# A layer norm, a spectral filter and a gated layer on one core: the filter's product one step later, its returns split, the last stage two tiles deep, fewer runs of zeros

## The chip, the cores and the metric

The kernel runs on one core of one Trainium2 chip. The metric is the time of the device in microseconds (us), start to end of one execution. A core has five engines with a queue of instructions each, taken in order: TensorE (PE; its weight loads are shown apart as PEld), VectorE (DVE), ScalarE (ACT), GpSimd (POOL) and SyncE (SP). Engines wait for each other through semaphores. DMA transfers are issued here by SP and by ACT.

## The reference

With x of 2048 rows and 512 columns in bf16, and xn the layer norm of x over its columns, the output is the sum of three terms:

```python
def _A_ref(x, w_r, w_i):
    X = rfft2(x.astype(float32))          # 2048 x 257, complex
    X = X * (w_r + 1j * w_i)
    return irfft2(X, s=(S, D)).astype(bfloat16)

def _B_ref(x, w_gate, w_up, w_down):      # 512 -> 1792 -> 512
    h = gelu(x @ w_gate) * (x @ w_up)
    return h @ w_down

xn = _layernorm(x)
return x + _A_ref(xn, w_r, w_i) + _B_ref(xn, w_gate, w_up, w_down)
```

## The kernel before

Everything is written out by hand. A small scheduler (`_Sched.op`) appends each operation to its engine's list in the order in which the program calls it, with the events that it must wait for; that order is each queue's order. A DMA counts on a named semaphore of its own.

The rows are held as 16 tiles of 128 rows, in four blocks of four. There are two streams of work, woven together.

*The gated layer* is made of units. A gate unit, `("g", block, fc)`, is two times four matmuls of 512 columns on PE (L504), a gelu on ACT (L516) and a product on DVE (L524) that writes hT. A down unit, `("d", block, n)`, is 14 matmuls (L552) that read all of the block's hT, and one add on DVE (L558). The units stand in one list, `fillers`, and `filler()` takes the next one. Gate units share a ring of three PSUM banks (0, 1, 2); down units of blocks 0 to 2 use bank 7, those of block 3 the gate units' ring.

*The spectral filter* is a two-dimensional transform made of matmuls, in stages:

- the first half, `unit_A` (L574) and `unit_d` (L600), one tile of 128 rows at a time through the buffers X1, stored to memory (`stage_p`) and read back in another order (`shuffle`);
- the middle, 16 units u of two groups each. `unit_B(u)`: two matmuls (L646), a copy by ACT into Xc (L651), and two DMAs on SP that write Xc with its halves of 64 partitions swapped into JX (L654). `product(u)`: three operations on DVE, M1 = Xc times wr (L663), JX = JX times wi (L664), M1 = M1 + JX (L665). `unit_c(u)`: two matmuls on M1 (L677), a copy by ACT into Vp (L682), and a store of Vp to memory (`stage_g`, L686) on SP;
- the return, `back(part)`: for each quarter of the groups, two DMAs (L696) that read `stage_g` back in another order into V, after the stores of that quarter;
- the last stage, per tile j: `unit_e(j)`, four matmuls (L710) and a copy by ACT into ZT (L715), and `unit_fin(j)`, four matmuls on ZT (L731), a copy by ACT (L738), two operations on DVE (L741, L742), one on DVE and one on POOL (L745), and the add into the output on POOL (L749). An output row is stored when both its down unit and its `unit_fin` have been added.

The middle runs in 19 steps. Step u has `unit_c(u-3)`, `unit_B(u)`, `product(u-2)`, one filler (steps 1 to 17), and after steps 8, 12 and 16 a return on ACT's queue; the last return is on SP's queue, behind the last step. Then come five fillers, and the last stage in 17 steps: `unit_e(j)`, `unit_fin(j-1)`, and a filler in steps 1 to 15. The four down units of block 3 are the end. `unit_B` and `unit_c` share four PSUM banks (3 to 6), two at a time. Xc and JX have three buffers, M1 and Vp two.

At the very start PE multiplies zeros by zeros into bank 7 (`warm_up`, L485) while the first rows are loaded and normed: NWARM gives the lengths of the runs, and each run after the first waits for an event of the norm (the statistics of tile 0, of tile 1, the reciprocal for both). The first real work are eight transposes (L441) and then gate units of 256 columns.

Of the kernel before, what the change touches and what calls it, by code (L numbers as in the profile page):

```python
# [7 lines left out]
ACT = mybir.ActivationFunctionType  # L8
ALU = mybir.AluOpType
# [5 lines left out]
HD = 256  # L15
NK = 257
FF = 1792
P = 128
NJ = 16
# [2 lines left out]
NFC = 14  # L22
NGG = 3
NX1 = 4
NWARM = (30, 6, 6, 5)
LN_EPS = 1e-5


# [123 lines left out]
class _Sched:  # L152
# [14 lines left out]
    def total(self, stream):  # L167
        return (stream, self.stream_cnt[stream])
# [59 lines left out]
def bass_parallel_sum__spectral_gfnet__glu_gated_geglu__prompt_kernel(  # L228
# [19 lines left out]
    sch = _Sched()  # L248

    with ExitStack() as es:  # L250

        def sb(name, shape, dt=BF16):
            return es.enter_context(nc.sbuf_tensor(name, shape, dt))
# [33 lines left out]
        V = bufB[:, :].rearrange("p (j c) -> p j c", j=NJ)  # L287
# [38 lines left out]

        streams = [("pe", 1), ("act", 1), ("dve", 1), ("pool", 1)]
        streams += [(n, 16) for n in ("x0", "x1", "x2", "x3", "xc1", "xc2", "xc3", "ident", "small", "fa", "eg", "wd", "wr", "wi",
                                      "w0", "w1", "w2", "w3", "dr0", "dr1", "perm1", "jx0", "jx1", "jx2", "vd0_0", "vd0_1", "vd1_0", "vd1_1", "vd2_0", "vd2_1", "vd3_0", "vd3_1", "perm2", "out")]
# [13 lines left out]
        spec = {}  # L343
# [29 lines left out]
        d2 = nc.dram_tensor("stage_g", [NG, P, NK], BF16).ap()  # L373
# [23 lines left out]
        ev_ag = {}  # L397
# [5 lines left out]
        ev_rstd = {}  # L403
# [160 lines left out]
        ev_X1 = {}  # L564
# [3 lines left out]
        def unit_A(j):  # L568
            slot, bdeps = ring_sp.alloc(1)

            def f_a(e):
                ins = None
                for r in range(4):
                    ins = e.matmul(sp_bank(slot)[:, r * P:(r + 1) * P], fold[:, r // 2, r % 2, j, :], AM[:, j, :], start=True, stop=True)  # L574
                return ins

            ev_p = sch.op("pe", f_a, deps=[ev_fa] + ev_fold[j // 4] + bdeps)
            spec["A_last"] = ev_p
            deps = [ev_p, X1_readers[j % NX1]]
            if j < 9:  # L580
                ev_X1[j] = sch.op("act", lambda e: e.activation(X1[j % NX1][:], sp_bank(slot), ACT.Copy), deps=deps)
            else:
                ev_X1[j] = sch.op("dve", lambda e: e.tensor_copy(X1[j % NX1][:], sp_bank(slot)), deps=deps)
            ring_sp.add_reader(slot, ev_X1[j])

        def clear_holes():
# [41 lines left out]
        Xc_readers = [[], [], []]  # L628
        JX_readers = [[], [], []]
        M_readers = [[], []]  # L630
        Vp_readers = [[], []]
        ev_Xc = {}
        ev_JX = {}
        ev_Y = {}
# [1 line left out]
        PARTS = ((0, 8), (8, 16), (16, 24), (24, 32))  # L636

        def unit_B(u):
            s3 = u % 3
            slot, bdeps = ring_sp.alloc(2)  # L640

            def f_b(e):
                ins = None
                for i in range(2):
                    g = 2 * u + i
                    ins = e.matmul(sp_bank(slot + i)[:, 0:NK], BM[:, 1 if g == 0 else 0, :], Tp[:, g, :], start=True, stop=True)  # L646
                return ins
# [3 lines left out]
            ev_Xc[u] = sch.op("act", lambda e: e.activation(Xc[s3][:], sp_pair(slot), ACT.Copy), deps=[ev_p] + Xc_readers[s3])  # L651
            ring_sp.add_reader(slot, ev_Xc[u], 2)
            for h in range(2):
                sch.op("sp", lambda e, h=h: e.dma_start(JX[s3][64 * h:64 * h + 64, :, :], Xc[s3][64 - 64 * h:128 - 64 * h, :, :]),  # L654
                       deps=[ev_Xc[u]] + JX_readers[s3], stream="jx%d" % s3)
            ev_JX[u] = total("jx%d" % s3)
            Xc_readers[s3] = [ev_JX[u]]

        def product(u):

            s2, s3 = u % 2, u % 3
            gs = slice(2 * u, 2 * u + 2)
            a = sch.op("dve", lambda e: e.tensor_tensor(M1[s2][:], Xc[s3][:], wr_sb[:, gs, :], ALU.mult), deps=[ev_Xc[u]] + M_readers[s2] + spec["wr"])  # L663
            b = sch.op("dve", lambda e: e.tensor_tensor(JX[s3][:], JX[s3][:], wi_sb[:, gs, :], ALU.mult), deps=[ev_JX[u], spec["neg"][u // 4]])  # L664
            ev_Y[u] = sch.op("dve", lambda e: e.tensor_tensor(M1[s2][:], M1[s2][:], JX[s3][:], ALU.add), deps=[a, b])  # L665
            Xc_readers[s3].append(a)
            JX_readers[s3] = [ev_Y[u]]

        def unit_c(u):
            s2 = u % 2  # L670
            slot, bdeps = ring_sp.alloc(2)

            def f_c(e):
                ins = None
                for i in range(2):
                    kind = 1 if 2 * u + i == 0 else 0
                    ins = e.matmul(sp_bank(slot + i)[:, 0:NK], CM[:, kind, :], M1[s2][:, i, :], start=True, stop=True)  # L677
# [4 lines left out]
            ev_v = sch.op("act", lambda e: e.activation(Vp[s2][:], sp_pair(slot), ACT.Copy), deps=[ev_p] + Vp_readers[s2])  # L682
            ring_sp.add_reader(slot, ev_v, 2)
            part = next(i for i, (lo, hi) in enumerate(PARTS) if lo <= 2 * u < hi)
            name = "vd%d_%d" % (part, s2)
            sch.op("sp", lambda e: e.dma_start(d2[2 * u:2 * u + 2].rearrange("g r k -> r g k"), Vp[s2][:]), deps=[ev_v], stream=name)  # L686
            Vp_readers[s2] = [total(name)]

        def back(part, eng):

            lo, hi = PARTS[part]
            ev = [total("vd%d_%d" % (part, i)) for i in range(2)]
            for pq in range(2):
                src = bass.AP(tensor=d2.tensor, offset=d2.offset + (lo * P + 16 * pq) * NK + pq,
                              ap=[[32 * NK, 4 * (hi - lo)], [NK, NJ], [1, HD]])
                sch.op(eng, lambda e, pq=pq, src=src: e.dma_start(V[4 * lo:4 * hi, :, pq * HD:(pq + 1) * HD], src),  # L696
                       deps=ev + [spec["A_last"]], stream="perm2")
            spec["perm2"] = total("perm2")

        ev_ZT = {}  # L700
# [213 lines left out]
```

## Time and profile before

| | us |
|---|---|
| runs | 186.41, 186.61, 186.67; median 186.61 |
| the profiled execution | 187.52 |
| its span, first to last instruction | 185.7 |
| PE busy in the stretch 60 to 78 (18.0 us) | 17.89 |
| PE busy in the middle, 78 to 124.5 (46.5 us) | 44.05 |
| of it 96 to 104 and 104 to 115 (8.0 and 11.0 us) | 6.98 and 10.04 |
| PE busy from 150 to 170 (20.0 us) | 19.84 |
| DVE, ACT, POOL busy in the middle (46.5 us) | 30.14, 25.97, 0.00 |
| DMA share in 84 to 96, 96 to 104, 104 to 115 | 0.40, 0.83, 0.63 |

A line of the profile's groups or of the order of time has a start and a duration in us, the engine, the line of the code, the operation, what is written and read with its shape, and in brackets the idle time of the engine before it and what ended it. "ACTq" and "SPq" are the engines' sequencers, which issue DMAs. Matmuls are pipelined: the start of one to the start of the next is its cost, and the duration shown is longer. The granted TensorE clock is 1.00 in each stretch that the profile reports, so the pace of the matmuls is read from their starts.

### The profile page before, as it was taken

What the parts mean: (1) busy time and instruction counts of PE and PEld (TensorE: products, weight loads), DVE (VectorE), ACT (ScalarE), POOL (GpSimd) and SP (SyncE); (2) the same over time, 40 slices, a digit from 0 to 9 for tenths busy, and PEclk for the clock granted to TensorE, in tenths of its full rate; (3) what the DMA queues carried; (4) which work ended last, traced back from release to release, by engine and by line L of the source; (5) the groups of instructions that cost most, each with busy time, mean ns of one, the idle gap of its engine ahead of it and who ended that gap; (6) DMA issues with size and microseconds to landing.
All of it is one profiled execution on the core that took longest, in us unless ns stands there. A gap on an engine that the chain in (4) does not pass through costs nothing.

```text
span 185.7 us, 3182 instructions
## 1 busy us (share of the span) xinstructions
PE 177.3 (95%) x1145; PEld 100.7 (54%) x1165; DVE 118.1 (64%) x252; ACT 88.6 (48%) x161; POOL 55.5 (30%) x54
## 2 busy tenths in 40 slices
PE   7999999999999999999999798999899999998994
PEld 6688555565655544545554453444455545554453
DVE  1767968799674636567585684733456858588221
ACT  2544446787463542267475472623453635465000
POOL 0064271373630000000000000000169778699500
PEclk9999999999999999999999999999999999999999
DMA  5999960999999584824349376545001021110001
GB/s 159 349 365 371 371 208 28 173 183 190 213 186 183 171 264 130 240 71 114 104 114 190 106 153 150 133 122 115 4 28 56 28 70 47 56 58 5 28 28 56
DMA packets 32224, 26.10 MB, mean 141 GB/s; under 512 B 2256, under 2 KB 31440, under 8 KB 32080
## 3 DMA queue, kind: packets, MB, share of 16 engines
q1 hardware_dynamic: 28368, 23.90, 49.4%
q10 hardware_dynamic: 3840, 2.00, 5.4%
q8 instruction: 9, 0.15, 0.3%
q14 instruction: 7, 0.06, 0.1%
HBM read 17.48 MB, written 6.30 MB: 128 GB/s over the span
## 4 chain that ended last, share of the span: by engine, by line
PE 82%; DMA 9%; DVE 4%; ACT 2%; issue 1%; SPq 1%; DVEq 0%
PE ps L504 46%; PE ps L552 23%; DMA JX<-Xc 7%; PE ps L441 2%; PE ps L731 2%; PE ps L574 2%; PE ps L600 2%; PE ps L710 2%; DMA x_sb<-in_A_x_dram 2%; PE ps L677 1%; DVE hT L524 1%; ACT Xc L651 1%; PE ps L485 1%; PE ps L646 1%; DVE M L665 1%
## 5 line engine op out<-in xcount | busy, mean ns | idle before, releaser
L504 PE MATMUL ps<-xnT,wu_sb 128*128 128x512 bf16 (+1 forms) x246 | 58.6, 361 | 0.1
L504 PE MATMUL ps<-xnT,wg_sb 128*128 128x512 bf16 (+1 forms) x233 | 56.4, 360 | 0.8
L524 DVE TENSOR_TENSOR hT<-ps,gg 128x512 bf16<-128x512 f32 (+1 forms) x62 | 39.5, 638 | 22.3 <-PE ps L504 21.1
L552 PE MATMUL ps<-wd_sb,hT 128*128 128x512 bf16 (+1 forms) x235 | 50.4, 367 | 0.8 <-DVE hT L524 0.6
L516 ACT ACTIVATE gg<-ps 128x512 bf16<-128x512 f32 (+1 forms) x62 | 34.4, 555 | 25.0 <-PE ps L504 23.9
L745 POOL TENSOR_TENSOR bufC<-bufC 128x256 bf16<-128x256 f32 x16 | 14.9, 931 | 86.5 <-DVE bufC L742 86.5
L504 PEld LDWEIGHTS ps<-xnT,wu_sb 128*128 128x128 bf16 x248 | 24.4, 99 | 24.3
L552 PEld LDWEIGHTS ps<-wd_sb,hT 128*128 128x128 bf16 x238 | 22.9, 98 | 23.4 <-DVE hT L524 0.8
L504 PEld LDWEIGHTS ps<-xnT,wg_sb 128*128 128x128 bf16 x248 | 23.2, 98 | 15.4 <-ACT xnT L450 0.2
L558 DVE TENSOR_TENSOR x_sb<-ps,x_sb 128x512 bf16<-128x512 f32 (+1 forms) x17 | 11.2, 660 | 24.2 <-PE ps L552 24.2
L465 POOL TENSOR_TENSOR bufC<-bufA 128x1024 bf16<-128x1024 bf16 x8 | 16.8, 2123 | 8.0 <-DVE bufA L423 8.0
L749 POOL TENSOR_TENSOR x_sb<-x_sb,bufC 128x512 bf16<-128x512 bf16 x16 | 18.5, 1154 | 2.3
L682 ACT ACTIVATE Vp<-ps 128x514 bf16<-128x514 f32 x16 | 9.6, 599 | 16.4 <-PE ps L677 14.3
L715 ACT ACTIVATE bufA<-ps 128x512 bf16<-128x512 f32 x16 | 9.4, 597 | 16.0 <-PE ps L710 16.0
L608 ACT ACTIVATE bufA<-ps 128x512 bf16<-128x512 f32 x16 | 11.9, 744 | 9.2 <-PE ps L600 9.2
L400 DVE BATCH_NORM_STATS2 st<-x_sb 128x6 f32<-128x512 bf16 x16 | 10.8, 678 | 3.1 <-DMA x_sb<-in_A_x_dram 3.1
L651 ACT ACTIVATE Xc<-ps 128x514 bf16<-128x514 f32 x16 | 9.4, 595 | 4.0 <-PE ps L646 4.0
L741 DVE TENSOR_TENSOR bufC<-bufC,ps 128x256 f32<-128x256 f32 x16 | 6.7, 421 | 6.4 <-ACT bufC L738 6.4
L664 DVE TENSOR_TENSOR JX<-JX,wi_sb 128x514 bf16<-128x514 bf16 x16 | 6.8, 424 | 5.7 <-DMA JX<-Xc 5.7
L677 PE MATMUL ps<-M,small 128*128 128x257 bf16 x32 | 6.2, 276 | 2.2 <-DVE M L665 2.2
L415 POOL TENSOR_SCALAR rstd<-ag 128x4 f32<-128x4 f32 (+1 forms) x4 | 1.6, 402 | 21.2 <-DVE ag L401 21.2
L745 DVE TENSOR_TENSOR bufC<-bufC 128x256 bf16<-128x256 f32 x16 | 7.2, 452 | 0.5
(42 smaller groups left out, 142.0 us busy)
## 6 DMA issues: line engine op xcount, KB each, us to landing
JX<-Xc SPq DMA_DIRECT2D x32, 64.2 KB, 2.3
stage_g<-Vp SPq DMA_DIRECT2D x16, 128.5 KB, 3.3
stage_p<-bufA SPq DMA_DIRECT2D x16, 128.0 KB, 7.8
bufC<-stage_p SPq DMA_DIRECT2D x4, 512.0 KB, 5.4
out_dram<-x_sb SPq DMA_DIRECT2D x15, 128.0 KB, 1.8
wd_sb<-in_B_w_down_dram SPq DMA_DIRECT2D x1, 1792.0 KB, 13.3
wr_sb<-in_A_w_r_dram SPq DMA_DIRECT2D x6, 257.0 KB, 6.5
wi_sb<-in_A_w_i_dram SPq DMA_DIRECT2D x6, 257.0 KB, 11.5
```

Of the source, the lines that this page charges most:

```text
L400: ev = sch.op("dve", lambda e: e.bn_stats(st[:, j, :], x_sb[:, j, :]), deps=[ev_x[j]])
L465: ev_hf[m] = [sch.op("pool", lambda e, t=t, op=op: e.tensor_tensor(half[:, m, t, :, :], rows[:, 0, :, :], rows[:, 1, :, :], op), deps=deps ...
L504: ins = e.matmul(gu_bank(slot)[:, 0:w], wsb[:, dc, fc * P:(fc + 1) * P], xnT[:, dc, b * 512 + a:b * 512 + a + w], start=(dc == 0), stop=(d ...
L516: ev_gg = sch.op("act", lambda e: e.activation(gg, gu_bank(gslot)[:, 0:w], ACT.Gelu_apprx_tanh), deps=[ev_gm] + gg_readers[s2])
L524: ev_h = sch.op("dve", lambda e: e.tensor_tensor(hT[hb][:, fc, a:a + w], gu_bank(uslot)[:, 0:w], gg, ALU.mult), deps=[ev_um, ev_gg] + hdeps)
L552: ins = e.matmul(bank(slot)[:, 0:w], hT[hb][:, fc, jj * P:(jj + 1) * P], wd_sb[:, fc, cs], start=(fc == 0), stop=(fc == NFC - 1))
L558: ev_a = sch.op("dve", lambda e, slot=slot, cs=cs: e.tensor_tensor(x_sb[:, j, cs], bank(slot)[:, 0:w], x_sb[:, j, cs], ALU.add), deps=[ev_ ...
L608: ev_T[j] = sch.op("act", lambda e: e.activation(dst, src, ACT.Copy), deps=[ev_p, tr[j]] + ev_hf[j // 4])
L651: ev_Xc[u] = sch.op("act", lambda e: e.activation(Xc[s3][:], sp_pair(slot), ACT.Copy), deps=[ev_p] + Xc_readers[s3])
L682: ev_v = sch.op("act", lambda e: e.activation(Vp[s2][:], sp_pair(slot), ACT.Copy), deps=[ev_p] + Vp_readers[s2])
L745: y = [sch.op(("dve", "pool")[h], lambda e, h=h, op=op: e.tensor_tensor(rS[s2][:, h * HD:(h + 1) * HD], yeS[s2][:, 0, :], yeS[s2][:, 1, :] ...
L749: ev_o = sch.op("pool", lambda e: e.tensor_tensor(x_sb[:, j, :], x_sb[:, j, :], rS[s2], ALU.add), deps=[a, b, ev_xn[j]] + ev_acc.get(j, []))
```

## The change

It has five parts.

1. The product of a unit comes three steps behind its transform and `unit_c` four: step u has `unit_c(u-4)`, `unit_B(u)`, `product(u-3)`. There are still 19 steps: step 16 has two products (13 and 14), step 17 one (15), step 18 two `unit_c` (14 and 15).
2. Xc and JX have four buffers and Vp three. The room for the fourth ones and for M1 comes from X1: one tile, `tmp`, holds X1's four buffers in the first half and afterwards M1, the fourth Xc and the fourth JX, as views.
3. A return's two DMAs are issued in two steps: after steps 9 and 10, 13 and 14, 17 and 18. The last return's two stay together on SP's queue.
4. The last stage runs `unit_fin(j-2)` beside `unit_e(j)`, in 18 steps, and the last down unit of block 2 stands behind all gate units of block 3 in the list of fillers, not before their last five.
5. The zeros are a run of 46, and one of 4 that waits for the reciprocal.

```diff
-NWARM = (30, 6, 6, 5)
+NWARM = (46, 4)
...
-        X1 = [sb("X1_%d" % i, [P, 512]) for i in range(NX1)]
+        tmp = sb("tmp", [P, 8 * NK])
...
-        Xc = [sb("Xc%d" % i, [P, 2, NK]) for i in range(3)]
-        JX = [sb("JX%d" % i, [P, 2, NK]) for i in range(3)]
-        M1 = [sb("M1_%d" % i, [P, 2, NK]) for i in range(2)]
-        Vp = [sb("Vp%d" % i, [P, 2, NK]) for i in range(2)]
+
+        X1 = [tmp[:, i * 512:(i + 1) * 512] for i in range(NX1)]
+        pairs = [tmp[:, i * 2 * NK:(i + 1) * 2 * NK].rearrange("p (a k) -> p a k", a=2) for i in range(4)]
+        M1 = pairs[0:2]
+        Xc = [sb("Xc%d" % i, [P, 2, NK])[:] for i in range(3)] + [pairs[2]]
+        JX = [sb("JX%d" % i, [P, 2, NK])[:] for i in range(3)] + [pairs[3]]
+        Vp = [sb("Vp%d" % i, [P, 2, NK]) for i in range(3)]
...
         def unit_B(u):
-            s3 = u % 3
+            s3 = u % 4
...
         def product(u):
 
-            s2, s3 = u % 2, u % 3
+            s2, s3 = u % 2, u % 4
...
         def unit_c(u):
-            s2 = u % 2
+            s2, sv = u % 2, u % 3
...
-        def back(part, eng):
+        def back(part, pq, eng):
 
             lo, hi = PARTS[part]
-            ev = [total("vd%d_%d" % (part, i)) for i in range(2)]
-            for pq in range(2):
-                src = bass.AP(tensor=d2.tensor, offset=d2.offset + (lo * P + 16 * pq) * NK + pq,
-                              ap=[[32 * NK, 4 * (hi - lo)], [NK, NJ], [1, HD]])
-                sch.op(eng, lambda e, pq=pq, src=src: e.dma_start(V[4 * lo:4 * hi, :, pq * HD:(pq + 1) * HD], src),
-                       deps=ev + [spec["A_last"]], stream="perm2")
+            src = bass.AP(tensor=d2.tensor, offset=d2.offset + (lo * P + 16 * pq) * NK + pq,
+                          ap=[[32 * NK, 4 * (hi - lo)], [NK, NJ], [1, HD]])
+            sch.op(eng, lambda e: e.dma_start(V[4 * lo:4 * hi, :, pq * HD:(pq + 1) * HD], src),
+                   deps=[total("vd%d_%d" % (part, i)) for i in range(3)] + [spec["A_last"]], stream="perm2")
             spec["perm2"] = total("perm2")
...
-        for n, ev in zip(NWARM, (None, ev_ag[0], ev_ag[1], ev_rstd[0])):
+        for n, ev in zip(NWARM, (None, ev_rstd[0])):
             warm_up(n, ev)
...
-                for n, at in enumerate((4, 7, 10, 13) if b < 3 else (3, 5, 7, 9)):
+                for n, at in enumerate((4, 7, 10, 13) if b < 3 else (3, 5, 7, 14)):
                     units.insert(at + n, ("d", b - 1, n))
...
         for u in range(19):
-            if u >= 3:
-                unit_c(u - 3)
+            for v in ((14, 15) if u == 18 else (u - 4,)):
+                if v >= 0:
+                    unit_c(v)
             if u < 16:
                 unit_B(u)
-            if 2 <= u < 18:
-                product(u - 2)
+            for v in {16: (13, 14), 17: (15,), 18: ()}.get(u, (u - 3,)):
+                if v >= 0:
+                    product(v)
             if 1 <= u < 18:
                 filler()
 
-            if u in (8, 12, 16):
-                back(u // 4 - 2, "act")
-        back(3, "sp")
+            if u in (9, 10, 13, 14, 17, 18):
+                back(u // 4 - 2, (u - 9) % 4, "act")
+        for pq in range(2):
+            back(3, pq, "sp")
         filler(todo["left"] - 15 - 4)
-        for j in range(NJ + 1):
+        for j in range(NJ + 2):
             if j < NJ:
                 unit_e(j)
-            if j >= 1:
-                unit_fin(j - 1)
+            if j >= 2:
+                unit_fin(j - 2)
             if 1 <= j < NJ:
                 filler()
         filler(todo["left"])
```

More of the change, by code (lines that the diff above doesn't have):

```diff
@@ L328, in bass_parallel_sum__spectral_gfnet__glu_gated_geglu__prompt_kernel @@
         streams += [(n, 16) for n in ("x0", "x1", "x2", "x3", "xc1", "xc2", "xc3", "ident", "small", "fa", "eg", "wd", "wr", "wi",
-                                      "w0", "w1", "w2", "w3", "dr0", "dr1", "perm1", "jx0", "jx1", "jx2", "vd0_0", "vd0_1", "vd1_0", "vd1_1", "vd2_0", "vd2_1", "vd3_0", "vd3_1", "perm2", "out")]
+                                      "w0", "w1", "w2", "w3", "dr0", "dr1", "perm1", "jx0", "jx1", "jx2", "jx3", "vd0_0", "vd0_1", "vd0_2", "vd1_0", "vd1_1", "vd1_2", "vd2_0", "vd2_1", "vd2_2", "vd3_0", "vd3_1", "vd3_2", "perm2", "out")]
         for name, inc in streams:
@@ L580, in unit_A @@
             if j < 9:
-                ev_X1[j] = sch.op("act", lambda e: e.activation(X1[j % NX1][:], sp_bank(slot), ACT.Copy), deps=deps)
+                ev_X1[j] = sch.op("act", lambda e: e.activation(X1[j % NX1], sp_bank(slot), ACT.Copy), deps=deps)
             else:
-                ev_X1[j] = sch.op("dve", lambda e: e.tensor_copy(X1[j % NX1][:], sp_bank(slot)), deps=deps)
+                ev_X1[j] = sch.op("dve", lambda e: e.tensor_copy(X1[j % NX1], sp_bank(slot)), deps=deps)
             ring_sp.add_reader(slot, ev_X1[j])
@@ L626, in negate @@
                 sch.op("dve", lambda e: e.tensor_scalar(w, w, -1.0, None, ALU.mult), deps=spec["wi"]))
-        Xc_readers = [[], [], []]
-        JX_readers = [[], [], []]
+        Xc_readers = [[] for _ in range(4)]
+        JX_readers = [[] for _ in range(4)]
         M_readers = [[], []]
-        Vp_readers = [[], []]
+        Vp_readers = [[], [], []]
         ev_Xc = {}
@@ L650, in unit_B @@
             spec["B_last"] = ev_p
-            ev_Xc[u] = sch.op("act", lambda e: e.activation(Xc[s3][:], sp_pair(slot), ACT.Copy), deps=[ev_p] + Xc_readers[s3])
+            ev_Xc[u] = sch.op("act", lambda e: e.activation(Xc[s3], sp_pair(slot), ACT.Copy), deps=[ev_p] + Xc_readers[s3])
             ring_sp.add_reader(slot, ev_Xc[u], 2)
@@ L659, in product @@
         def product(u):
-            s2, s3 = u % 2, u % 3
+            s2, s3 = u % 2, u % 4
             gs = slice(2 * u, 2 * u + 2)
-            a = sch.op("dve", lambda e: e.tensor_tensor(M1[s2][:], Xc[s3][:], wr_sb[:, gs, :], ALU.mult), deps=[ev_Xc[u]] + M_readers[s2] + spec["wr"])
-            b = sch.op("dve", lambda e: e.tensor_tensor(JX[s3][:], JX[s3][:], wi_sb[:, gs, :], ALU.mult), deps=[ev_JX[u], spec["neg"][u // 4]])
-            ev_Y[u] = sch.op("dve", lambda e: e.tensor_tensor(M1[s2][:], M1[s2][:], JX[s3][:], ALU.add), deps=[a, b])
+            a = sch.op("dve", lambda e: e.tensor_tensor(M1[s2], Xc[s3], wr_sb[:, gs, :], ALU.mult), deps=[ev_Xc[u]] + M_readers[s2] + spec["wr"])
+            b = sch.op("dve", lambda e: e.tensor_tensor(JX[s3], JX[s3], wi_sb[:, gs, :], ALU.mult), deps=[ev_JX[u], spec["neg"][u // 4]])
+            ev_Y[u] = sch.op("dve", lambda e: e.tensor_tensor(M1[s2], M1[s2], JX[s3], ALU.add), deps=[a, b])
             Xc_readers[s3].append(a)
@@ L681, in unit_c @@
             M_readers[s2] = [ev_p]
-            ev_v = sch.op("act", lambda e: e.activation(Vp[s2][:], sp_pair(slot), ACT.Copy), deps=[ev_p] + Vp_readers[s2])
+            ev_v = sch.op("act", lambda e: e.activation(Vp[sv][:], sp_pair(slot), ACT.Copy), deps=[ev_p] + Vp_readers[sv])
             ring_sp.add_reader(slot, ev_v, 2)
             part = next(i for i, (lo, hi) in enumerate(PARTS) if lo <= 2 * u < hi)
-            name = "vd%d_%d" % (part, s2)
-            sch.op("sp", lambda e: e.dma_start(d2[2 * u:2 * u + 2].rearrange("g r k -> r g k"), Vp[s2][:]), deps=[ev_v], stream=name)
-            Vp_readers[s2] = [total(name)]
-        def back(part, eng):
+            name = "vd%d_%d" % (part, sv)
+            sch.op("sp", lambda e: e.dma_start(d2[2 * u:2 * u + 2].rearrange("g r k -> r g k"), Vp[sv][:]), deps=[ev_v], stream=name)
+            Vp_readers[sv] = [total(name)]
+        def back(part, pq, eng):
             lo, hi = PARTS[part]
-            ev = [total("vd%d_%d" % (part, i)) for i in range(2)]
-            for pq in range(2):
-                src = bass.AP(tensor=d2.tensor, offset=d2.offset + (lo * P + 16 * pq) * NK + pq,
-                              ap=[[32 * NK, 4 * (hi - lo)], [NK, NJ], [1, HD]])
-                sch.op(eng, lambda e, pq=pq, src=src: e.dma_start(V[4 * lo:4 * hi, :, pq * HD:(pq + 1) * HD], src),
-                       deps=ev + [spec["A_last"]], stream="perm2")
+            src = bass.AP(tensor=d2.tensor, offset=d2.offset + (lo * P + 16 * pq) * NK + pq,
+                          ap=[[32 * NK, 4 * (hi - lo)], [NK, NJ], [1, HD]])
+            sch.op(eng, lambda e: e.dma_start(V[4 * lo:4 * hi, :, pq * HD:(pq + 1) * HD], src),
+                   deps=[total("vd%d_%d" % (part, i)) for i in range(3)] + [spec["A_last"]], stream="perm2")
             spec["perm2"] = total("perm2")
```

## The prediction

> **What bounds the kernel now.** I read the page first, for the share of TensorE, then the list of who waited for whom, kept to TensorE, then the order of time at each place where it waited.
>
> ```profile
> PE 177.3 (95%) x1145; PEld 100.7 (54%) x1165; DVE 118.1 (64%) x252; ACT 88.6 (48%) x161; POOL 55.5 (30%) x54
> ...
> PE ps L677 <- DVE M L665: 2.2, 3, 1.0
> ...
> PE ps L552 <- DVE hT L524: 0.6, 1, 0.6
> ...
> PE ps L731 <- ACT bufA L715: 0.5, 1, 0.5
> ```
>
> TensorE is busy 177.3 of 185.7 us, so only two things can shorten the run: its idle time and the time in which its matmuls are slow. The list (us in total, times, longest) has 2.2 us before three L677 products, 0.6 before the last down products, 0.5 before the first L731, and beside these only waits of the zeros (L485) at the start. Next, the order of time at a product wait.
>
> ```profile
> 96.43 0.93 ACTq L696 DMA_DIRECT2D bufB<-stage_g  x2
> 96.45 1.10 SPq L654 DMA_DIRECT2D JX<-Xc  x2
> ...
> 102.90 0.43 DVE L664 TENSOR_TENSOR JX<-JX,wi_sb 128x514 bf16<-128x514 bf16 x1 [2.42 <-DMA JX<-Xc]
> 103.36 0.43 DVE L665 TENSOR_TENSOR M<-M,JX 128x514 bf16<-128x514 bf16 x1
> 103.71 0.68 DVE L558 TENSOR_TENSOR x_sb<-ps,x_sb 128x512 bf16<-128x512 f32 x1
> 103.85 0.40 PE L677 MATMUL ps<-M,small 128*128 128x257 bf16 x2 [0.97 <-DVE M L665]
> ```
>
> ACT issues two returns (L696) in the same moment as SP issues the swap of one unit (L654). That swap lands after 5.2 and 5.9 us; the first swap, with no return near, took 2.0. VectorE waits 2.42 us for it and TensorE 0.97 after that. The second pair of returns (107.55) repeats it with 0.91; 0.30 is lost at the first product of all.
>
> **The change, part by part.**
>
> *Product three steps behind, four buffers, split returns.* The swap of unit u is issued up to 2.0 us into its step (second half at 96.95, step begun at 94.91) and multiplied some 1.15 us into the step of its product. Two ordinary steps of 2.17 us leave 3.5 us, and 5.9 does not fit: 2.4 us of waiting, as shown. With three steps, one of which holds a down product (3.46 us) for every unit near the first two pairs of returns, 6.9 us are left, so even an unsplit 5.9 fits. The first product gets a whole extra step. Gain 2.2, bounds 1.3 (one wait stays) and 2.2 (no more is there). The matmuls are the same, and the extra buffers cost no instruction. Splitting moves one DMA issue of each pair past one more step on ACT; the issue (0.3 to 0.6 us on ACT's sequencer) lies beside the running gelu.
>
> A rule of the Trainium skill speaks against the split: its page "DMA: Bandwidth & Descriptors", in "Issuing engines are not separate DMA queues", says that transfers of all issuing engines end up on the same 16 DMA engines and interleave. The 5.9 us of the swap on SP behind ACT's returns agrees. By that rule alone the split returns would slow twice as many swaps half as much and be worth nothing; the sum here gives the split nothing either, since the third step covers both.
>
> *The seam, steps 16 to 18.* The lag has to be made up: step 16 now has two products (units 13 and 14), step 17 the last, step 18 two L677 pairs. VectorE runs in order, and each step's gate product (L524) waits for TensorE. The spacing is that of these rows:
>
> ```profile
> 117.30 0.69 DVE L524 TENSOR_TENSOR hT<-ps,gg 128x512 bf16<-128x512 f32 x1 [0.70 <-PE ps L504]
> 117.91 0.42 DVE L663 TENSOR_TENSOR M<-Xc,wr_sb 128x514 bf16<-128x514 bf16 x1
> 118.24 0.42 DVE L664 TENSOR_TENSOR JX<-JX,wi_sb 128x514 bf16<-128x514 bf16 x1
> 118.69 0.43 DVE L665 TENSOR_TENSOR M<-M,JX 128x514 bf16<-128x514 bf16 x1
> ```
>
> L524 starts 0.21 after TensorE's step ends (117.09); then +0.61, +0.33, +0.45 to the three product operations, +0.35 from an L665 to the next operation (103.36 to 103.71). Let T be TensorE's start of step 16. VectorE: L524 of step 15 at T+0.21, product 13 from 0.82 (its L665 ends at 2.03), product 14 from 1.95 (ends 3.16), L524 of step 16 at 3.08, product 15 from 3.69, its L665 ends at 4.90. TensorE: L677 pair 0.22, gate and up products to 1.95; the next pair waits for 2.09; gate and up to 4.04; pair 14 to 4.26; pair 15 waits for 4.96 and ends at 5.18. Before, this stretch with one pair fewer ran from 117.09 to 121.36, 4.27 us; with the fourth pair 4.49. Cost 5.18 - 4.49 = 0.7. The bounds: 0.35 if half the queue hides, and 1.3, because the swap of unit 15 follows a return. It is multiplied at T+4.02, its second half is issued near T-0.55, and the swap that followed two returns by one step (109.7 to 110.2) took up to 5.2, which would be T+4.65, 0.6 late.
>
> *The last return.* It follows the last pair on SP and now competes with both returns of the third part. Before, the last store (122.26) took 2.7, the later half of the last return (125.35) landed 4.5 after its issue, at 129.9, and the last stage began at 131.29: 1.4 us of cover. After: from the last pair's start 1.05 to the store's issue, 3.4 for the store (the value of the one at 118.14, which had two returns behind it), 0.4 for the second issue, 4.5: 9.4 us. The last stage begins 10.15 after that start (121.14 to 131.29). Cover 0.8, cost 0. With the slowest store between returns (109.25, 5.8) it is 11.75, cost 1.6. Bounds 0 and 1.6; I take 0, by the nearer row. Third store buffers only end waits of ACT (1.6 us at 90.79) on which TensorE did not wait.
>
> *Two tiles ahead, and the last of block 2's down products moved to the end.*
>
> ```profile
> 131.72 1.09 ACT L715 ACTIVATE bufA<-ps 128x512 bf16<-128x512 f32 x2 [0.49 <-PE ps L710]
> 132.37 0.40 PE L731 MATMUL ps<-fa,bufA 128*128 128x128 bf16 x4 [0.47 <-ACT bufA L715]
> 170.22 0.68 DVE L524 TENSOR_TENSOR hT<-ps,gg 128x512 bf16<-128x512 f32 x1
> 170.96 1.25 PE L552 MATMUL ps<-wd_sb,hT 128*128 128x512 bf16 x5 [0.64 <-DVE hT L524]
> ```
>
> The first L731 now comes 3.02 us of down products later than the copy of its input: 0.5 gone. The last L524 gets the same 3.02 us of cover ahead of the final down products: 0.6 gone. What follows a step later is POOL's tail: two tiles of about 2.17 us behind the start of the final products, done some 5.3 us in, when the add for the last tile is 10.8 us in (170.96 to 181.76). Without that cover POOL's 2.17 would count in full.
>
> *Zeros: 46 and 4 for 30, 6, 6 and 5.*
>
> ```profile
> 0.97 3.38 PE L485 MATMUL ps<-hT 128*128 128x128 bf16 x30 [0.97 <-DVE hT L394]
> 4.98 2.15 PE L485 MATMUL ps<-hT 128*128 128x128 bf16 x17 [0.62 <-DVE ag L401]
> 8.84 1.06 PE L504 MATMUL ps<-xnT,wu_sb 128*128 128x256 bf16 x4
> 9.69 0.67 PE L504 MATMUL ps<-xnT,wg_sb 128*128 128x256 bf16 x4
> 10.19 0.60 PE L504 MATMUL ps<-xnT,wu_sb 128*128 128x256 bf16 x4
> 10.63 0.60 PE L504 MATMUL ps<-xnT,wg_sb 128*128 128x256 bf16 x4
> ```
>
> Four matmuls take 0.85 us from 8.84 and 0.44 from 10.19: the array reaches full pace near 9.7, some 4.7 us after work with no long gap began (4.98). The 46 zeros run at 0.11 each from 0.97 to about 6.0, unbroken for 5 us, before the reciprocal that the last four await (6.25), so nothing is delayed. If 4.7 us are what it needs, full pace is there before the real work; about 0.9 us of slow matmuls fall away, but the second piece of the up weights, issued at 3.59, lands 7.5 later, at 11.07, and its user started at 11.50: at most 0.43 gained. If instead the two new gaps (near 6.0 and before 7.16) make the count start anew at 7.16, full pace comes at 11.9, and 2.2 us at 0.48 lost per us cost 1.05. Bounds -0.43 and +1.05; I take -0.2, between nothing and the weights' limit.
>
> The Trainium skill's page "TensorE: Matmul & The Clock Gate" (section "Part 1: The HAM clock gate") describes a free-running window of about 3.4 us that must be busy. By it, a run of 5 us holds a whole window only for some phases, and the sum would move by anything from -0.43 to nothing for the phase drawn; no run here shows the window itself.
>
> **Sum.** -2.2 - 0.5 - 0.6 + 0.7 + 0 - 0.2 = -2.8. Against the profiled execution's 187.52 (185.7 of span, 1.8 around it) that gives 184.7. The median of the runs, 186.61, lies 0.9 lower; I carry the difference over: **183.8**.
>
> **Rivals.** *Seam and last return cost their upper ends* (chance 0.17): SP, ACT and the returns are closer together than before, which the 5.8 us store at 109.25 speaks for and the 3.4 at 118.14 against. +1.6 gives 185.4, with the late swap's 0.6 it is 186.0. *The clock comes later* (0.08): +1.05 instead of -0.2 gives 185.05. *The waits stay* (0.05): the third step covers nothing, because swaps land later than 6.9 us; no row is above 5.9. The 1.9 of the two waits come back: 185.7. *VectorE becomes the bound* (0.08), the slower side: M1 and the fourth Xc and JX lie in one shared tile at odd multiples of 1028 bytes. If the three product operations there took the 0.68 of the 512-wide copies from ps (L583) instead of 0.42, each product grows by 0.78 against 0.34 of idle per step; ten ordinary steps lose 4.4, the seam 2.3: 190.5. It is slower than before from 0.48 per product on (10 x (0.48 - 0.34) + 3 x 0.48 = 2.8). Against it: wr_sb and wi_sb are read at such multiples, and all 16 of each of L663 and L664 took 417 to 429 ns.
>
> **How the numbers follow.** The forecast has 0.62 (183.0 to 184.6 with its own terms). For 8 in 10 the range goes up into the first two rivals and down past the full 0.43 of the zeros: 182.9 to 185.6. A change within 0.2%, 0.37 us, can't be told from none. All cases but the last are faster by more; the last holds slower 0.07 and, with partial slowing, same 0.03; faster 0.90.
>
> **What would show it.** Right: no L664 wait for JX, L677 waits of 0.1 and 0.7 only in steps 17 and 18, no wait of L731 or of L552 for L524, four 256-wide matmuls in 0.44 us before 9. Wrong: an L710 wait for the last return, L663 to L665 above 0.43, or a slow pace beyond 10.

## The result, and the profile after

The changed kernel takes 183.42 us (median of 182.99 to 183.68, 4 runs) against 186.64 (186.41 to 186.92) for the kernel before: ratio 0.9824, 95% interval 0.9801 to 0.9848, so 3.2 us less. The prediction was 183.8 with a range of 182.9 to 185.6.

The page of the changed kernel (first line) and its list of TensorE's waits (us in total, times, longest); the line numbers have moved by 3, L677 is now L680, L664 is L667:

```profile
PE 175.1 (97%) x1148; PEld 99.8 (55%) x1168; DVE 117.3 (65%) x252; ACT 88.5 (49%) x161; POOL 55.5 (31%) x54
...
PE ps L488 <- DVE hT L397: 1.0, 1, 1.0
PE ps L680 <- DVE tmp L668: 0.5, 1, 0.5
PE ps L444 <- DVE bufA L426: 0.5, 1, 0.5
PE ps L507 <- DMA wu_sb<-in_B_w_up_dram: 0.5, 1, 0.5
```

Of the three waits of the product one is left, and it is at another place (the seam, below). The waits before the first L731 and before the last down products are gone. Two new ones have come at the start: the transposes (L444) wait for the normed rows, and a gate unit (L507) waits for the up weights.

The span fell by 4.5 us (185.7 to 181.2), more than the medians' 3.2. Cut at three marks that both traces have (lines as they were before), the first L646 (78.16 before, 76.98 after), the first L710 (131.29, 128.25) and the first down product of block 3 (170.96, 166.48), the start gave 1.2, the middle 1.85, the last stage 1.44 and the end nothing. Most of the 1.2 of the start is not the change's. The fourth gate unit reads the second piece of the up weights, and it started at 11.50 before and 10.31 after. That piece, unchanged work, landed at 11.08 in the one execution and 10.26 in the other: 0.8. The other 0.4 is the slow pace of TensorE in the execution profiled before, whose first rows also came late: they landed 3.27 us after their issue (at 3.98), after the change 2.35 (3.07). What the two other stretches gave, 3.3, is the 3.2 of the medians. The profiled execution of before lay 0.9 above the median of its runs, and this start is where: the prediction's carrying that 0.9 over was right.

The swaps, in order of time, at a return of the changed kernel (start, duration, engine, line):

```profile
96.87 0.34 ACTq L697 DMA_DIRECT2D bufB<-stage_g  x1
96.89 1.10 SPq L657 DMA_DIRECT2D JX<-Xc  x2
...
104.31 0.42 DVE L667 TENSOR_TENSOR JX<-JX,wi_sb 128x514 bf16<-128x514 bf16 x1
```

The swap of unit 9 starts beside one half of a return. Its two halves land 4.2 and 4.8 us after their issues, the later at 102.2, and the swap is used at 104.31: no bracket, so no wait.

The seam (steps 16 to 18, where the longer lag is made up), first VectorE, then TensorE, each in order of time:

```profile
113.34 0.69 DVE L527 TENSOR_TENSOR hT<-ps,gg 128x512 bf16<-128x512 f32 x1 [0.35 <-PE ps L507]
...
114.74 0.43 DVE L668 TENSOR_TENSOR tmp<-tmp,JX 128x514 bf16<-128x514 bf16 x1
...
115.87 0.43 DVE L668 TENSOR_TENSOR tmp<-tmp,JX 128x514 bf16<-128x514 bf16 x1
116.22 0.68 DVE L527 TENSOR_TENSOR hT<-ps,gg 128x512 bf16<-128x512 f32 x1
...
117.61 0.43 DVE L668 TENSOR_TENSOR tmp<-tmp 128x514 bf16<-128x514 bf16 x1
```

```profile
113.14 0.39 PE L680 MATMUL ps<-tmp,small 128*128 128x257 bf16 x2
...
115.22 0.40 PE L680 MATMUL ps<-tmp,small 128*128 128x257 bf16 x2
...
117.18 0.39 PE L680 MATMUL ps<-tmp,small 128*128 128x257 bf16 x2
118.09 0.40 PE L680 MATMUL ps<-tmp,small 128*128 128x257 bf16 x2 [0.52 <-DVE tmp L668]
118.33 0.38 PE L555 MATMUL ps<-wd_sb,hT 128*128 128x512 bf16 x1
```

With T, the start of step 16 on TensorE, at 113.14, the three L668 start at T+1.60, T+2.73 and T+4.47, the pairs of L680 at T+2.08, T+4.04 and T+4.95, and the stretch ends at T+5.19. The last pair waits for VectorE, whose queue has two products behind one L527; seam14, below, tests this.

The last stage begins like this:

```profile
128.25 0.61 PE L711 MATMUL ps<-fa,bufB 128*128 128x128 bf16 x8
128.70 3.19 PE L555 MATMUL ps<-wd_sb,hT 128*128 128x512 bf16 x14
131.72 0.39 PE L711 MATMUL ps<-fa,bufB 128*128 128x128 bf16 x4
131.94 0.39 PE L732 MATMUL ps<-fa,bufA 128*128 128x128 bf16 x4
```

There is no wait at the first L711 (the last return landed at 127.23, 1.0 earlier) and none at the first L732. The first two lines also show how a wait is to be counted: the eight L711 are given 0.61 us, but the next matmul starts 0.45 after the first of them. The shown end holds some 0.16 of pipeline that the next matmul does not wait for. The idle time in a bracket is counted from that end, so it leaves out 0.16 of every wait.

### The profile page after: what moved, and what is told of

It reads as the page before. It is cut to its first block, busy times and chain, and to the rows that moved or that the text cites. A ratio compares the mean times of both kernels' runs of the same rounds, so it can differ in the third digit from the quotient of the medians.

```text
span 181.2 us, 3176 instructions
## 1 busy us (share of the span) xinstructions
PE 175.1 (97%) x1148; PEld 99.8 (55%) x1168; DVE 117.3 (65%) x252; ACT 88.5 (49%) x161; POOL 55.5 (31%) x54
## 4 chain that ended last, share of the span: by engine, by line
PE 90%; DMA 4%; DVE 3%; SPq 1%; issue 1%
PE ps L507 50%; PE ps L555 27%; DMA wu_sb<-in_B_w_up_dram 4%; PE ps L577 2%; PE ps L732 2%; PE ps L711 2%; PE ps L603 2%; PE ps L649 2%; PE ps L680 2%; PE ps L444 2%; SPq L339 1%; DVE hT L527 1%; DVE tmp L666 1%; DVE tmp L668 0%; DVE JX L667 0%
## 5 line engine op out<-in xcount | busy, mean ns | idle before, releaser
L507 PE MATMUL ps<-xnT,wu_sb 128*128 128x512 bf16 (+1 forms) x246 | 58.3, 358 | 0.1
L507 PE MATMUL ps<-xnT,wg_sb 128*128 128x512 bf16 (+1 forms) x234 | 56.2, 357 | 1.3 <-DMA wu_sb<-in_B_w_up_dram 0.5
L527 DVE TENSOR_TENSOR hT<-ps,gg 128x512 bf16<-128x512 f32 (+1 forms) x62 | 39.5, 638 | 21.7 <-PE ps L507 20.5
L746 POOL TENSOR_TENSOR bufC<-bufC 128x256 bf16<-128x256 f32 x16 | 14.7, 917 | 85.5 <-DVE bufC L743 85.5
L507 PEld LDWEIGHTS ps<-xnT,wu_sb 128*128 128x128 bf16 x248 | 24.2, 98 | 24.2
L507 PEld LDWEIGHTS ps<-xnT,wg_sb 128*128 128x128 bf16 x248 | 22.9, 98 | 16.0 <-DMA wu_sb<-in_B_w_up_dram 0.7
L654 ACT ACTIVATE Xc<-ps 128x514 bf16<-128x514 f32 x12 | 7.0, 595 | 4.0 <-PE ps L649 4.0
L584 ACT ACTIVATE tmp<-ps 128x512 bf16<-128x512 f32 x9 | 5.4, 597 | 4.5 <-PE ps L577 4.5
L739 ACT ACTIVATE bufC<-ps 128x256 f32<-128x256 f32 x16 | 6.0, 378 | 2.6 <-PE ps L732 2.6
```

What stands on the lines that cost most here:

```text
L507: ins = e.matmul(gu_bank(slot)[:, 0:w], wsb[:, dc, fc * P:(fc + 1) * P], xnT[:, dc, b * 512 + a:b * 512 + a + w], start=(dc == 0), stop=(d ...
L527: ev_h = sch.op("dve", lambda e: e.tensor_tensor(hT[hb][:, fc, a:a + w], gu_bank(uslot)[:, 0:w], gg, ALU.mult), deps=[ev_um, ev_gg] + hdeps)
L746: y = [sch.op(("dve", "pool")[h], lambda e, h=h, op=op: e.tensor_tensor(rS[s2][:, h * HD:(h + 1) * HD], yeS[s2][:, 0, :], yeS[s2][:, 1, :] ...
```

## The experiments

Each kernel was run beside the kernel before on the same chip, in three groups; ratios have 95% intervals. "Lost" is the time that TensorE lost to waits from the first L680 or L677 on, counted from start to start in the profiled execution.

| kernel | median us | ratio to before | lost us |
|---|---|---|---|
| before (first profile) | | | 4.2 |
| group 1, before 187.08 | | | |
| zeros_back | 183.28 | 0.9788 [0.9763, 0.9813] | 0.96 |
| lag2_split | 183.60 | 0.9824 [0.9787, 0.9862] | 2.7 |
| lag3_whole | 183.39 | 0.9794 [0.9769, 0.9819] | 0.96 |
| seam14 | 182.67 | 0.9761 [0.9737, 0.9785] | 0.43 |
| group 2, before 186.43 | | | |
| after_again | 183.26 | 0.9829 [0.9806, 0.9852] | 0.96 |
| lag2_whole | 185.36 | 0.9941 [0.9921, 0.9961] | 3.15 |
| last_stage_back | 184.55 | 0.9895 [0.9874, 0.9916] | 2.4 |
| seam16 | 182.94 | 0.9806 [0.9781, 0.9832] | 0.83 |
| group 3, before 186.66 | | | |
| seam17 | 182.80 | 0.9799 [0.9784, 0.9813] | 0.14 |
| zeros_alone | 186.75 | 1.0009 [0.9992, 1.0026] | 5.0 |
| late_new | 186.57 | 0.9991 [0.9974, 1.0008] | 0.96 |
| late_old | 185.48 | 0.9937 [0.9923, 0.9952] | 0.96 |

**The changed kernel again (after_again)**, the control of group 2. 

> The changed kernel itself, beside the others of this group, so that they are compared on one chip. Every theory: a ratio to the kernel before between 0.980 and 0.985, as first measured, or a little below it where the kernel before runs slower.

It repeats the first result.

**The third step and the returns.** Parts 1 and 3 undone in their order of work (lag2_whole):

```diff
-            for v in ((14, 15) if u == 18 else (u - 4,)):
-                if v >= 0:
-                    unit_c(v)
+            if u >= 3:
+                unit_c(u - 3)
...
-            for v in {16: (13, 14), 17: (15,), 18: ()}.get(u, (u - 3,)):
-                if v >= 0:
-                    product(v)
+            if 2 <= u < 18:
+                product(u - 2)
...
-            if u in (9, 10, 13, 14, 17, 18):
-                back(u // 4 - 2, (u - 9) % 4, "act")
+            if u in (8, 12, 16):
+                for pq in range(2):
+                    back(u // 4 - 2, pq, "act")
```

> The changed kernel with parts 1 and 3 undone in their order of work: product two steps behind, both DMAs of a return after steps 8, 12 and 16; the extra buffers, the last stage and the zeros stay as changed. Theory A (the two parts together are worth the three waits, counted from start to start 0.47 + 1.14 + 1.08, less the seam's 0.83): 1.7 to 1.9 above the changed kernel. Rival B (the extra buffers alone end the waits): no more than 0.3 above it.

2.1 us above the control of its group (185.36 to 183.26; the intervals of the ratios lie far apart). The order of time at its first return (of its two DMAs the second is shown):

```profile
95.59 1.10 SPq L657 DMA_DIRECT2D JX<-Xc  x2
...
95.94 0.56 ACTq L697 DMA_DIRECT2D bufB<-stage_g  x1
...
102.19 0.43 DVE L667 TENSOR_TENSOR JX<-JX,wi_sb 128x514 bf16<-128x514 bf16 x1 [2.56 <-DMA JX<-Xc]
...
103.13 0.40 PE L680 MATMUL ps<-tmp,small 128*128 128x257 bf16 x2 [1.10 <-DVE tmp L668]
```

The swap issued at 95.59 beside the return lands 5.0 and 6.1 us after its issues, at 102.16, and VectorE waits for it. The waits are back with all the buffers in place, so buffers alone end nothing; its lost time is 3.15 against 0.96, a difference of 2.2. Rival B fell. The 2.1 is a little above theory A's 1.9 because the two waits at returns cost 1.27 and 1.28 in this execution.

Then each of the two parts alone: lag2_split is the first two hunks without the third, lag3_whole only this:

```diff
-            if u in (9, 10, 13, 14, 17, 18):
-                back(u // 4 - 2, (u - 9) % 4, "act")
+            if u in (9, 13, 17):
+                for pq in range(2):
+                    back(u // 4 - 2, pq, "act")
```

lag2_split: 

> The changed kernel with the product two steps behind again (unit_c three), four buffers and split returns kept. Theory A (the third step is what covers the swaps): VectorE waits some 2 us for two swaps again, TensorE loses about 1.1 twice and 0.5 at the first product, the seam's 0.8 is gone: 183.4 + 2.7 - 0.8 = 185.3. Rival B (the split returns and their place beside the down-product steps cover them alone): the units whose swap meets a return (9, 10, 13) have one down-product step among their two, which leaves 4.7 us, and the swaps landed 4.5 to 4.9 after their issue in the changed kernel: VectorE waits 0.2 at most, TensorE loses 0.5 at the first product and nothing at the seam: 183.4 + 0.4 - 0.8 = 183.0.

lag3_whole: 

> The changed kernel with each return's two DMAs together again, after steps 9, 13 and 17, the product still three steps behind. Theory A (the third step alone covers the swaps): swaps land up to 5.9 us after issue against 6.9 of cover, no wait of L667 for JX, 183.4 within 0.2. Rival B (the split is needed as well): L667 waits for JX come back at units 9 and 13, 0.5 to 1.1 of TensorE each: 184.4 to 185.5.

lag3_whole is theory A to the letter: no L667 waits for JX, though its swap at 97.3 took 6.2 us to land. lag2_split is neither. Its median lies 0.2 to 0.3 above zeros_back and lag3_whole of its group, but its six runs go from 183.12 to 185.41, while lag3_whole's stay within 0.6. The profile is of the slowest run; its waits, of VectorE and of TensorE:

```profile
DVE JX L667 <- DMA JX<-Xc: 2.6, 4, 1.5
PE ps L680 <- DVE tmp L668: 1.9, 3, 1.3
```

Split returns beside the down-product steps leave 4.7 us, and here the swaps near them landed after 5.3 and 6.3 us, where the changed kernel's took 4.8 and 4.9 in its first profile. In the profile of after_again, the same program, they took 4.9 and 6.1: that length is not peculiar to the lag of two. Four of the six runs lie within 183.12 to 183.62, which suggests that the swaps landed soon enough there; those runs have no profile. So the split with its place ends most of the waits too, but on the edge; the third step, with 6.9 us, covers them whether the returns are split or not, and costs the seam.

**The seam.** The lag made up in step 14, which has a down product and a VectorE with time:

```diff
-            for v in {16: (13, 14), 17: (15,), 18: ()}.get(u, (u - 3,)):
+            for v in {14: (11, 12), 15: (13,), 16: (14,), 17: (15,), 18: ()}.get(u, (u - 3,)):
```

> The changed kernel with the lag made up two steps earlier: products 11 and 12 both in step 14, which has a down product and so a VectorE with time, product 13 in step 15, 14 in step 16, 15 in step 17; unit_c as changed. Theory A (the wait of 0.7 before the last L680 pair and the 0.14 before the one of step 17 are VectorE's queue, two products behind one gate product): both go, no new wait, 183.4 - 0.8 = 182.6. Rival B (the last return would have ended that wait): the last stage's first L711 waits instead, 183.4. Rival C (the swap of unit 13, now two steps before its product, is late): a wait of L667 at unit 13 of up to 0.5, 183.1.

182.67, 0.6 to 0.7 below zeros_back and lag3_whole of its group. No L680 waits in steps 16 to 18, so the wait was VectorE's queue. Of rival C there is one wait of VectorE for a swap, of 0.2, which costs TensorE nothing; but rival B holds in part:

```profile
126.76 1.03 PE L507 MATMUL ps<-xnT,wu_sb 128*128 128x512 bf16 x4
127.92 0.62 PE L711 MATMUL ps<-fa,bufB 128*128 128x128 bf16 x8
```

Four matmuls of 512 columns cost 0.86, so L711 could have started at 127.62. It lost 0.3, because the last return landed at 127.87. Its store, issued at 118.78 behind another store and half a return, took 4.6 us. Two kernels spread these out:

```diff
-            for v in ((14, 15) if u == 18 else (u - 4,)):
+            for v in {17: (13, 14), 18: (15,)}.get(u, (u - 4,)):
...
-            if u in (9, 10, 13, 14, 17, 18):
-                back(u // 4 - 2, (u - 9) % 4, "act")
+            for v in {9: (0,), 10: (1,), 13: (0,), 14: (1,), 17: (0, 1)}.get(u, ()):
+                back(u // 4 - 2, v, "act")
```

on top of seam14's line is seam17; seam16 has units 12 and 13 in step 16, 14 in step 17.

seam16: 

> As seam14 (products 11 and 12 in step 14), with the lag of unit_c made up as well: units 12 and 13 in step 16, 14 in step 17, 15 in step 18, and the third return's two DMAs both after step 17. Theory A (what seam14 still lost at the first L711, 0.3, was the last return, held up by two stores and a return issued in the same microsecond): no wait at the first L711, 0.14 at the last L680, 0.8 to 1.0 below the changed kernel. Rival B (the last return is late for another reason): the wait of 0.3 stays, 0.6 below it.

seam17: 

> As seam14 (products 11 and 12 in step 14), with units 13 and 14 of unit_c in step 17 and 15 in step 18, and the third return's two DMAs both after step 17. Theory A (seam14's wait of 0.3 at the first L711 came from the last return crowded by stores and a return, and seam16's 0.56 from asking for unit 13 one step too early): neither wait, 0.14 at most in steps 17 and 18, 0.7 to 0.9 below the changed kernel, 182.4 to 182.6. Rival B: the last return is late all the same, 0.3 at the first L711, 182.9.

In seam16 the wait at L711 is gone, as theory A had it, but the pair of unit 13, asked for one step sooner, loses 0.56: its swap landed after 5.6 us and VectorE waited 0.8 for it. Its median is 0.3 below the control, not 0.8, and the intervals of the two overlap. seam17 has neither wait and loses 0.14 in all:

```profile
115.74 0.61 PE L680 MATMUL ps<-tmp,small 128*128 128x257 bf16 x4
116.19 1.02 PE L507 MATMUL ps<-xnT,wg_sb 128*128 128x512 bf16 x4
117.05 1.03 PE L507 MATMUL ps<-xnT,wu_sb 128*128 128x512 bf16 x4
117.91 0.39 PE L680 MATMUL ps<-tmp,small 128*128 128x257 bf16 x2
```

Every line starts where the one before it stops costing. Its ratio, 0.9799 [0.9784, 0.9813], is below the changed kernel's 0.9829 and 0.9824, some 0.5 us and not the 0.7 to 0.9 expected; seam14's is 0.9761 against 0.9788 and 0.9794 beside it. The intervals overlap a little in both cases, and seam17 had no changed kernel beside it on its chip. That both gain rests on the traces as well: 0.43 and 0.14 lost, against 0.96. Which of the two is better was not run on one chip and stays open.

**The last stage (last_stage_back).**

```diff
-                for n, at in enumerate((4, 7, 10, 13) if b < 3 else (3, 5, 7, 14)):
+                for n, at in enumerate((4, 7, 10, 13) if b < 3 else (3, 5, 7, 9)):
...
-        for j in range(NJ + 2):
+        for j in range(NJ + 1):
...
-            if j >= 2:
-                unit_fin(j - 2)
+            if j >= 1:
+                unit_fin(j - 1)
```

> The changed kernel with part 4 undone: one tile ahead, and the last down unit of block 2 before the last five gate units. Theory A (each wait costs the distance from start to start, 0.63 before the first L732 and 0.80 before the last down products): 1.4 above the changed kernel; from the first L711 to the first L555 of block 3 39.7 us in its profile against 38.2. Rival B (they cost the idle time that the profile shows, 0.47 and 0.64): 1.1. Rival C (the POOL tail takes part of it back in the changed kernel): under 0.8.

```profile
128.44 0.61 PE L711 MATMUL ps<-fa,bufB 128*128 128x128 bf16 x8
129.52 0.40 PE L732 MATMUL ps<-fa,bufA 128*128 128x128 bf16 x4 [0.47 <-ACT bufA L716]
...
168.11 1.25 PE L555 MATMUL ps<-wd_sb,hT 128*128 128x512 bf16 x5 [0.64 <-DVE hT L527]
```

1.3 us above the control. From 128.44 to 168.11 it is 39.67, in the changed kernel 38.23: 1.44, which is theory A; the brackets sum to 1.11. The times alone (1.3) do not tell A from B, the traces do. Rival C fell: from the first down product of block 3 to the end it is 14.7 us in both, so POOL's tail takes nothing back.

**The zeros.** zeros_back is the changed kernel with the old runs, zeros_alone the kernel before with the new:

```diff
-NWARM = (46, 4)
+NWARM = (30, 6, 6, 5)
...
-        for n, ev in zip(NWARM, (None, ev_rstd[0])):
+        for n, ev in zip(NWARM, (None, ev_ag[0], ev_ag[1], ev_rstd[0])):
```

zeros_back: 

> The changed kernel with the old zeros (30, 6, 6 and 5), all else as changed. Theory A (46 unbroken zeros bring full pace before the first real matmul, but the second piece of the up weights then ends the wait, so little is kept): full pace near 9 to 10 us again, no wait for the weights before the fourth unit, time 0.2 to 0.5 above the changed kernel's 183.42, so 183.6 to 183.9. Rival B (the zeros are worth the whole 0.9 us of slow matmuls): 184.3. Rival C (the clock's release does not follow the zeros): 183.4, and the same early full pace as in the changed kernel's profile.

zeros_alone: 

> The kernel before with the new zeros (46 and 4) and nothing else of the change. Theory A (the second piece of the up weights ends the start in nearly every execution, whatever the clock): within 0.3 of the kernel before. Rival B (the zeros are worth the 0.2 to 0.4 of the prediction): 0.2 to 0.4 faster. Rival C (worth the whole slow stretch): 0.9 faster.

Neither moves the time: 183.28 beside 183.39 with the new zeros (lag3_whole), and 1.0009 on the kernel before. (The lost time of zeros_alone, 5.0 against 4.2 with the middle unchanged, shows how far the waits for swaps differ between two executions.) In zeros_back the first rows landed at 3.04, so the second run of zeros followed the first without a gap, and full pace was there near 5 us with the old zeros too. And whatever the pace, the start ends with the same transfer. The chain of the changed kernel that ends in the first 14 us:

```profile
3.59 6.67 DMA wu_sb<-in_B_w_up_dram
10.26 0.05 issue
10.31 1.05 PE ps L507 x8
```

The unit that reads the second piece of the up weights started at 10.1 to 11.0 us in the profiles of groups 1 and 2 and of zeros_alone and seam17, in each of them 0.05 us after that piece had landed.

Late rows, made by issuing the first gate weights first, with the new zeros (late_new) and with the old (late_old):

```diff
         for j in range(4):
+            if j == 0:
+                load_w(0, (0,))
             ev_x[j] = load("x%d" % j, x_sb[:, j, :], xv[:, j, :])
-            if j == 1:
-                load_w(0, (0,))
```

late_new: 

> The changed kernel with the first gate weights issued ahead of the first rows, so that the rows land about 1 us later; zeros 46 and 4. Theory A (an unbroken run of zeros brings full pace by itself): full pace at or before the first transposes, as in the changed kernel; the start ends with a wait for the up weights as before, so the time is within 0.5 of 183.3. Rival B (the pace follows the rows' arrival): slow transposes and slow first gate units.

late_old: 

> The same late rows with the old zeros (30, 6, 6, 5). Theory A (a gap after the 30 zeros, which the late rows make, restarts what the clock counts): a gap of 0.6 or more after the 30 zeros, slow transposes and slow first gate units, full pace near 9 to 11, time 0.3 to 1.0 above the one with 46. Rival B (gaps do not matter): full pace as early as with 46, and the same time.

None of these theories holds, and the edit overshot: the rows landed at 5.8 and 5.6, some 2.6 us late, and both kernels are 2 to 3 us slower than the changed one. With the new zeros the kernel is 1.1 us slower than with the old. The stretches of late_new (busy time of PE, PEld, DVE, ACT, POOL with instructions, granted clock, DMA share, GB/s):

```profile
3.00:6.30 3.30, 3.06 (x29) 2.79 (x27) 0.45 (x1) 0.06 (x1) 0.00 (x0) 1.00 1.09 354
6.40:9.70 3.30, 1.00 (x12) 0.69 (x12) 2.38 (x9) 2.06 (x4) 0.00 (x0) 1.00 1.09 361
9.80:13.10 3.30, 3.30 (x16) 2.28 (x17) 1.99 (x6) 1.05 (x4) 0.96 (x2) 0.50 1.08 356
13.20:16.60 3.40, 3.40 (x37) 3.10 (x36) 2.24 (x7) 1.64 (x4) 2.10 (x2) 1.00 1.03 385
```

(The record of the clock begins at 6.34; the 1.00 of the first row stands for no record. The 46 zeros ran 0.107 us apart there, the last four, under the full clock, 0.06.) The 46 zeros did bring the full clock, from 6.34 on; then TensorE had 12 matmuls in 3.4 us, and the clock was halved from 9.75 to 13.17, on real matmuls. In late_old the same happened earlier: full from 4.28, half from 7.69 to 11.10, of which only 1.4 us had real gate products.

```profile
4.30:7.60 3.30, 0.69 (x10) 0.47 (x10) 1.71 (x4) 0.15 (x1) 0.00 (x0) 1.00 1.07 337
7.70:11.10 3.40, 3.26 (x26) 2.27 (x23) 2.56 (x8) 2.62 (x6) 0.00 (x0) 0.50 1.06 377
```

In these two profiles the place of the half clock is nearly all of the difference: the first group of gate matmuls back at full pace is the fifth in late_new (13.11) and the third in late_old (11.26), and late_old's fifth starts at 12.13, 1.0 earlier. That it goes so in every execution is not shown. All four runs of late_old and seven of the ten of late_new have a granted clock of 0.991, which is one such stretch. One run of late_new has 0.982, and two have 1.00, no half stretch on record, and were no faster (186.92 and 186.87). The runs of the two kernels do not overlap (185.76 to 187.40, 185.24 to 185.67).

## Why the prediction held, point by point

- *Product three steps behind.* Right in mechanism, and right that the split adds nothing to it (lag3_whole). Too small in size: "Gain 2.2, bounds 1.3 (one wait stays) and 2.2 (no more is there)". The three waits cost 0.47, 1.14 and 1.08 from start to start, 2.7, because brackets leave out the tail. That the split and its place would nearly do the same without the third step was not seen. The rule of the Trainium skill weighed there (page "DMA: Bandwidth & Descriptors", "Issuing engines are not separate DMA queues") says that transfers interleave, and swaps beside one half of a return did still take 4.1 to 6.1 us in the two profiles of the changed kernel, against 2.0 with no return near. Beside a whole return they took 5.0 to 6.2 (lag3_whole). By these figures the split and the place beside a longer step each leave some of the room; no run has the one without the other at a lag of two, so their shares are not shown.
- *The seam.* 0.7 by the sum, T+5.18 for its end: T+5.19 measured, and seam14 takes it away by undoing the queue alone. Worth noting is that the prediction's times of VectorE's operations were each right within 0.01 to 0.02 us; counted from start to start, rows of one execution carry over to another order. One reading in its upper bound was off: the second half of unit 15's swap was put near T-0.55, and the rows have it at T-0.12 before and T-0.13 after, so a landing after 5.2 would have been 1.0 late and not 0.6. It played no part, since that swap landed in 2.1 us.
- *The last return.* Cost 0, cover 0.8: 1.0 of cover measured. That this cover is thin showed in seam14, which had 0.3 less than none.
- *Last stage.* 0.5 + 0.6 = 1.1: 1.3 by the times, 1.44 by the trace. The same mis-sized term.
- *The zeros.* -0.2: nothing (zeros_alone 1.0009, [0.9992, 1.0026]). The limit named there, the up weights, is the whole answer. The step that failed is that their user "started at 11.50" was taken for the usual start, when in that execution the rows were 0.9 late and the old zeros had a gap that they do not have when the rows land at 3.0 (zeros_back). That unbroken zeros bring full pace by themselves was right: they did, in ten of the eleven profiles with 46, by the first transposes. In the eleventh, after_again, the transposes still ran at 0.106 us each and the full clock came at 7.00. The 4.7 us read from one execution are no fixed need: all these zeros begin at 0.97, and full pace came 2.8 to 6.0 us later.
- *Sum.* -2.8, measured -3.2 (2.8 to 3.7 by the interval of the ratio). Five waits (0.47, 1.14, 1.08, 0.63 and 0.80 from start to start, 4.1 in all) were given 3.3: 0.8 more gain. The zeros' 0.2 did not come. That makes -3.4; the lost time of the two traces, 4.2 and 0.96, makes -3.3. That the forecast lies within 0.4 of the result is thus in part luck: an undersized gain and a gain that did not come lie on opposite sides. The rivals' prices were not needed: no late return, no clock late enough to cost anything, and VectorE's operations in the shared tile take 416 to 429 ns, as before (the four views start at 0 to 3 times 1028 bytes, so only two of them at odd multiples).

## What to carry to other kernels

Count a wait from the start of the matmul before it, less what that matmul costs, and not by the idle time shown: here each was 0.16 us longer. When a loop's lag is made longer, plan where it is made up: put the doubled work into a step whose many matmuls leave the other engine idle, not into the last, shortest ones. Before tuning the first microseconds, look which transfer ends them, and in more than one execution.

## What was not expected of the hardware

The clock's stretches come in windows: late_new's clock went full at 6.34, half at 9.75 and full at 13.17 us, late_old's full at 4.28, half at 7.69, full at 11.10, each 3.41 apart. In the eleven profiles that begin with 46 zeros at 0.97, full pace came anywhere between 3.74 (seam17) and 7.00 us (after_again), a spread of 3.3, as it would if the windows do not start with the kernel. The Trainium skill's page "TensorE: Matmul & The Clock Gate" ("Part 1: The HAM clock gate") gives such a window, and a throttle after an idle one; here a window with a third of its time shown busy (1.00 of 3.30 us) was idle enough, though the longest gap between two matmuls was 2.3 us. One run of zeros followed by a wait was here worse than zeros spread over it: 186.57 against 185.48 us.

The first load's landing differs by 1.0 us between executions of unchanged work (2.27 us after issue in after_again, 3.27 in the first profile of the kernel before), which is more than twice the 0.43 that the zeros could have gained by the prediction.
